# Pooled attention of four early head pairs with heads on halves of the partitions, and value blocks requested by ScalarE

## The chip, the cores and the metric

The kernel runs on one NeuronCore of one Trainium2 chip. The core has five engines with an instruction queue each, worked off in order: TensorE (PE, with its weight loads shown as PEld), VectorE (DVE), ScalarE (ACT), GpSimd (POOL) and SyncE (SP), which here only requests DMA transfers. The metric is the device time of one execution in microseconds, as the median of several runs.

## The reference

Inputs are q, k and v of shape 8 x 8 x 576 x 64 (batch, heads, positions, channels), a token mixing U (576 x 32) and V (32 x 576), and two feed-forward matrices (512 x 2048 and 2048 x 512), all float32.

```python
q_d = q.reshape(B, H, Sd, 4, D).mean(axis=3)      # k_d and v_d likewise, Sd = 144
out_d = sm_attn(q_d, k_d, v_d)                    # softmax attention of the pooled rows
out_up = np.repeat(out_d, 4, axis=2)
mask = np.abs(pos[:, None] - pos[None, :]) < 4
...                                               # softmax attention within the mask, with v
x = (out_up + out_local)                          # to B x S x 512
u = x + ((x.transpose(0, 2, 1) @ U) @ V).transpose(0, 2, 1)
return u + np.maximum(u @ w_ch1, 0.0) @ w_ch2
```

So each head has a pooled attention over 144 rows and a local one over a band of seven neighbours. Their sum is mixed over the tokens at rank 32, and a feed-forward network follows.

## The kernel before

Work is emitted as small operations to a planner (`Plan`, lines 55 to 200). Each operation has an engine, an estimated duration, what it reads and writes, and a priority. The planner simulates the five engines and one DMA stream, takes on each engine the ready operation of the lowest priority number, and emits all operations in the order of the simulated starts. On the chip each engine then follows that order, and waits where the data is not there yet. The estimates therefore set the order, and the chip sets the times.

Heads are handled in pairs, with the 64 channels of the first head on partitions 0 to 63 and those of the second on 64 to 127. Batch 0, the first four pairs, takes an "early" way that stays in on-chip memory (`early_global`, `local_blocks`, `early_mix`); the other 28 pairs take a "late" way through DRAM (`late_global`, `local_attn`, `mix_part`). The feed-forward (`ffn1`, line 941, and `ffn2`, line 966) runs over thirteen token tiles, four of 288 and nine of 384, in 16 slices of the hidden dimension each, and begins when batch 0 is mixed.

Pooled attention of an early pair (`early_global`, lines 442 to 514): GpSimd pools q, k and v (lines 437, 439, 454, 457). The 144 queries are cut in two groups of 72, which lie on 72 partitions. Line 468 makes the scores of both heads into two PSUM banks of the pool `ps_m`, which has two. Then for each head there are a maximum (475), a scaled copy of it (478) and two exponentials with sums (483); later, one head after the other, four transposes (497), a copy (501), the product with v (508) and a scaling (511) into `od`.

Local attention of an early pair (`local_blocks`) has band scores (line 609, on a mask laid by 621), a softmax (629 to 642), transposes (652, copied by 654), and the product with the value block `vw` (664), copied out by ACT as `ob` (668). There is one `vw` buffer for all four pairs, so that the request for a pair's block (`load_vw`, line 595) waits for line 664 of the pair before. All DMA requests stand in SP's queue.

`early_mix` brings `od` and `ob` under the channels (686, 687, 693), adds them (696), makes U's product (705 for the local part, 707 for the pooled part with a pooled U made once, lines 385 and 388), splits it (710, 711, 714) and applies V (723, 727). Lines 730 and 732 split the result into the two parts that the feed-forward reads.

Weights of the feed-forward come raw (line 414) and are converted by ACT (347), DVE (350, 352), ACT (358) and GpSimd (362), 32 of them, between all of this and the early part of the feed-forward. The first requests of batch 1 (gq, line 589) need the memory of the early buffers and wait until the last early operation has ended.

The late pooled attention (lines 537 to 577) puts the heads on halves of the partitions: three groups of 48 queries, head 0 on partitions 0 to 63 and head 1 on 64 to 127. Line 775 makes the scores in blocks of 32 queries, 541 takes the maximum of both heads, 543 and 545 follow, 556 transposes 128 x 128, and 559, 571 and 575 close it.

Of the kernel before, what the change touches and what calls it, by code (L numbers as in the profile page):

```python
# [203 lines left out]
def attn_mix_ffn_kernel(ctx: ExitStack, tc, q, kp, vp, qT, kT, v, U, Ub, V, w1, w2, band, eye, pool, vw, ident, outT):  # L204
# [30 lines left out]
    NOD = 3  # L235
# [7 lines left out]
    KV = vw.shape[2]  # L243

# [12 lines left out]
    def psum(pool, name, tag, bufs):  # L257
        return buf(pool, [128, 512], F32, name, tag, bufs)
# [48 lines left out]
    Upool = early_pool.tile([128, 2, 2 * R], F32, name="Upool")  # L307
# [65 lines left out]
    def load_ublk(prio):  # L373
        raw = raw_in(NFC - 1, "ubr")
        dma(lambda raw=raw: nc.sync.dma_start(
            out=raw().bitcast(U16)[:, :4 * NS * R - 1], in_=Ub.bitcast(U16)[:, 1:]), [], [raw], prio, 164)
        convert(raw, 128, NS * R, lambda: Ublk[:, :, 0:R], None, NS, "Ub", "cu", prio)
        pool_sb = buf(wts, [128, 144], F32, "pool", f"W2_{NFC - 5}:pool")
        dma(lambda: nc.sync.dma_start(out=pool_sb(), in_=pool), [], [pool_sb], prio, 74)
        pu = psum(ps_acc, "ps_p", "acc1:p", 1)  # L380
        u4 = lambda: pu()[:QH, :2 * R].rearrange("p (a r) -> p a r", a=2)

        def u_mm():
            for n, (r, a) in enumerate(CROSS):
                nc.tensor.matmul(u4()[:, a], pool_sb()[:, 64 - QL * r + QH * a:64 - QL * r + QH * a + QH], Ublk[:, r, 0:R],
                                 start=(n == 0), stop=(n == len(CROSS) - 1))
        op(PE, 0.7, u_mm, ["UbH", pool_sb], [pu], prio)
        act(2 * R, lambda: nc.scalar.activation(Upool[:QH, :, 0:R], u4(), AF.Copy), [pu], ["Up"], prio, 0.16)
# [43 lines left out]
    CROSS = ((0, 0), (1, 0), (2, 0), (2, 1), (3, 1), (4, 1))  # L432

# [8 lines left out]
    def early_global(b, hp, prio, qt, kt):  # L442
        sq = work(True, glo, [128, SD], F32, "smq")
# [3 lines left out]
        od = ring([2, 2, D], "od_e", NOD)  # L447
        vs = ring([4 * D], "vs_e")
# [12 lines left out]
        view = lambda t, n: t()[:QH, :2 * n].rearrange("p (a k) -> p a k", a=2)  # L461
        rs = work(True, glo, [QH, 2, 2], F32, "rs")
        ps = psum_pair(ps_m, "ps_s", "m:g", 2)

        def s_mm():
            for a in range(2):
                for hh, o in enumerate(heads):
                    nc.tensor.matmul(view(ps[hh], SD)[:, a], sq()[o, a * QH:(a + 1) * QH], sk()[o],
                                     start=True, stop=True)
        op(PE, pw(prio) * 1.4, s_mm, [sq, sk], ps, prio)  # L470
        Es = []
        for hh in range(2):
            p = ps[hh]
            mx = work(True, glo, [QH, 2], F32, "mx")
            dve(288, lambda p=p, mx=mx: nc.vector.tensor_reduce(
                out=mx(), in_=view(p, SD), axis=AX.X, op=ALU.max), [p], [mx], prio)
            nb = work(True, glo, [QH, 2], F32, "nb")
            act(2, lambda mx=mx, nb=nb: nc.scalar.activation(
                nb(), mx(), AF.Copy, scale=-1.0 / 128.0), [mx], [nb], prio, 0.16)
            E = ring([2, SD], "E_e")  # L480
            Es.append(E)
            for a in range(2):
                act(SD, lambda a=a, hh=hh, E=E, p=p, nb=nb: nc.scalar.activation(
                    E()[:QH, a, :], view(p, SD)[:, a, :], AF.Exp, bias=nb()[:, a:a + 1], scale=1.0 / 128.0,
                    accum_out=rs()[:, hh, a:a + 1]), [p, nb], [(E, a), (rs, a, hh)], prio, 0.237)
        rr = work(True, glo, [QH, 2, 2], F32, "rr")
        act(4, lambda: nc.scalar.activation(rr(), rs(), AF.Copy, bias=4e-9, scale=4.0),
            [(rs, a, hh) for a in range(2) for hh in range(2)], [rr], prio, 0.16)
        ri = work(True, glo, [QH, 2, 2], F32, "ri")
        dve(24, lambda: nc.vector.reciprocal(out=ri(), in_=rr()), [rr], [ri], prio)  # L490
        for hh in range(2):
            pt = psum(ps_m, "ps_t", "m:g", 2)

            def t_mm(hh=hh, pt=pt):
                for c in range(2):
                    for a in range(2):
                        nc.tensor.transpose(view(pt, SD)[:, c, a * QH:(a + 1) * QH],
                                            Es[hh]()[:QH, a, c * QH:(c + 1) * QH], ident_sb[:QH, :QH])
            op(PE, pw(prio) * 0.48, t_mm, [(Es[hh], 0), (Es[hh], 1), "ident"], [pt], prio)
            ET = Es[hh]  # L500
            act(288, lambda ET=ET, pt=pt: nc.scalar.activation(ET()[:QH], view(pt, SD), AF.Copy),
                [pt], [(ET, 0), (ET, 1)], prio, 0.05)
            pa = psum(ps_m, "ps_a", "m:g", 2)

            def a_mm(ET=ET, pa=pa, v=vsx[hh]):
                for a in range(2):
                    for c in range(2):
                        nc.tensor.matmul(view(pa, D)[:, a, :], ET()[:, c, a * QH:(a + 1) * QH],
                                         v()[:, c, :], start=(c == 0), stop=(c == 1))
            op(PE, pw(prio) * 0.95, a_mm, [(ET, 0), (ET, 1), vs], [pa], prio)  # L510
            dve(128, lambda pa=pa, hh=hh: nc.vector.tensor_tensor(
                out=od()[:QH, :, hh, :], in0=view(pa, D),
                in1=ri()[:, hh, :].unsqueeze(2).broadcast_to([QH, 2, D]), op=ALU.mult), [pa, ri], [(od, hh)], prio)
# [78 lines left out]
    def load_vw(b, h0, prio):  # L592
        vw_t = ring([NL + 2, D], "vw", 1)
        for hh in range(2):
            dma(lambda hh=hh: nc.sync.dma_start(
                out=vw_t()[hh * KW:hh * KW + KV, 0:NL], in_=vw[b * HP + h0 // 2, hh]), [], [(vw_t, hh)], prio, 221)
# [77 lines left out]
    def early_mix(b, hp, x, od, prio):  # L674
        rd = [(x, g) for g in range(2)] + [(od, g) for g in range(2)]
        up = lambda a: od()[:, a].rearrange("p h d -> p (h d)")
# [7 lines left out]
        def od_t():  # L684
            for a in range(2):
                nc.tensor.transpose(pc()[:, q4 - SD + a * QH:q4 - SD + (a + 1) * QH], up(a)[:QH], ident_sb[:QH, :QH])
            nc.tensor.transpose(pc()[:, :S - q4], flat(4)[:S - q4], ident_sb[:S - q4, :S - q4])
# [15 lines left out]
        def hu():  # L703
            for n in range(NS):
                nc.tensor.matmul(ph()[:2 * R, :2 * D], Ublk[:, n, :], flat(n), start=(n == 0), stop=False)
            for a in range(2):
                nc.tensor.matmul(ph()[:2 * R, :2 * D], Upool[:, a, :], up(a), start=False, stop=(a == 1))
        op(PE, 1.6, hu, rd + ["UbH", "Up"], [ph], prio)
# [34 lines left out]
    QC, NQ = 48, 3  # L743
# [345 lines left out]
```

## Time and profile before

| | us |
|---|---|
| median of three runs | 1007.88 |
| lowest and highest | 1006.73 and 1010.25 |
| profiled execution | 1009.96 |
| its span, first to last instruction | 1008.2 |
| busy in it: PE, DVE, ACT, POOL | 973.4, 440.4, 349.6, 572.3 |

The page gives busy time by engine, the chain of work that ended last (followed back from the end, each step to what released it), and groups of equal instructions with count, busy time, mean duration, idle time before them and what ended it. Views of the trace give stretches of time (windows), instructions in order of time, and waits by engine. `L664` is line 664 of the kernel. A matmul of float32 shows as two instructions, a transpose as one. A name ending in q, as SPq, is the queue of that engine, where DMA requests are issued.

The granted clock averages 0.99 over the span.

### The profile page before, as it was taken

How to read it: one execution, taken by the hardware profiler on the slowest of the kernel's cores; microseconds unless marked ns; L12 is line 12 of the kernel's file. 1: busy time of each engine (PE TensorE's matmuls, PEld its weight loads, DVE VectorE, ACT ScalarE, POOL GpSimd, SP SyncE). 2: the span in 40 equal slices, each digit the busy share in tenths (PEclk: the TensorE clock that was granted, in tenths of full speed). 3: DMA queues.
4: the chain of work that ended last, by engine and by line, in shares of the span. 5: the costliest groups of instructions: out<-in, count | busy, mean ns of one | idle time of the engine just before them, and what ended most of it. 6: DMA issues, size and time to landing. Idle time of an engine off the chain costs nothing.

```text
span 1008.2 us, 24256 instructions
## 1 busy us (share of the span) xinstructions
PE 973.4 (97%) x9724; PEld 944.7 (94%) x9724; DVE 440.4 (44%) x824; ACT 349.6 (35%) x1023; POOL 572.3 (57%) x641
## 2 busy tenths in 40 slices
PE   5979999799999999999999999999999999999998
PEld 4769899799899999999999999999999999999998
DVE  5666855535453543642635444454363222211211
ACT  5766644333343333432433333433331221111110
POOL 6677897867766764864867866766764111300100
PEclk9989999989999999999999999999999999999999
DMA  9678867656564645655554565465541021000000
GB/s 280 170 243 228 260 147 152 142 129 159 108 152 105 171 92 124 147 129 125 147 129 104 145 150 127 111 161 123 123 121 54 13 68 24 32 1 1 32 1 31
DMA packets 220648, 120.01 MB, mean 119 GB/s; under 512 B 173988, under 2 KB 196856, under 8 KB 220536
## 3 DMA queue, kind: packets, MB, share of 16 engines
q1 hardware_dynamic: 220536, 118.47, 47.2%
q8 instruction: 76, 1.25, 0.5%
q14 instruction: 36, 0.29, 0.1%
HBM read 87.57 MB, written 30.86 MB: 117 GB/s over the span
## 4 chain that ended last, share of the span: by engine, by line
PE 80%; DMA 4%; POOL 4%; DVE 2%; issue 1%; SPq 1%; ACT 1%; DVEq 0%; POOLq 0%
PE ps_h L941 36%; PE acc L966 35%; PE ps_a L571 2%; POOL Pt L837 2%; PE ps_b L775 2%; PE ps_hu L916 2%; DMA ul<-up_s 1%; PE ps_t L556 1%; PE ps_b L768 1%; DMA s_s<-se 1%; DVE acc L842 1%; PE ps_u L723 1%; POOL W L362 1%; DMA gT<-in_kT 1%; SPq L791 1%
## 5 line engine op out<-in xcount | busy, mean ns | idle before, releaser
L966 PE MATMUL acc<-hH,W 128*128 128x384 f32 (+1 forms) x1664 | 441.9, 327 | 0.0
L941 PE MATMUL ps_h<-uH,W 128*128 128x384 f32 (+1 forms) x1376 | 360.4, 324 | 5.3 <-DVE hL L950 5.3
L966 PEld LDWEIGHTS acc<-hH,W 128*128 128x128 f32 x1664 | 297.4, 188 | 2.2
L966 PE MATMUL acc<-hL,W 128*128 128x384 f32 (+1 forms) x832 | 268.2, 322 | 0.0
L837 POOL TENSOR_TENSOR Pt<-vl,ms 128x896 f32<-128x896 f32 (+1 forms) x140 | 239.4, 1789 | 43.9 <-DMA vl<-in_vp 23.9
L950 DVE SCALAR_TENSOR_TENSOR hL<-ps_h,hH 128x384 fp32r<-128x384 f32 (+1 forms) x208 | 109.1, 524 | 342.6 <-ACT hH L949 342.6
L941 PEld LDWEIGHTS ps_h<-uH,W 128*128 128x128 f32 x1376 | 246.4, 190 | 7.5 <-DVE hL L950 6.3
L949 ACT ACTIVATE hH<-ps_h 128x384 fp32r<-128x384 f32 (+1 forms) x208 | 97.2, 467 | 378.3 <-PE ps_h L941 370.3
L941 PE MATMUL ps_h<-uL,W 128*128 128x384 f32 (+1 forms) x688 | 221.6, 322 | 1.4 <-POOL uL L732 1.4
L842 DVE TENSOR_REDUCE acc<-Pt 128x128 f32<-128x1024 f32 (+1 forms) x140 | 152.8, 1107 | 55.0 <-POOL Pt L837 28.0
L966 PEld LDWEIGHTS acc<-hL,W 128*128 128x128 f32 x832 | 156.7, 188 | 0.0
L941 PEld LDWEIGHTS ps_h<-uL,W 128*128 128x128 f32 x688 | 130.8, 190 | 1.6 <-POOL uL L732 1.6
L941 PE MATMUL ps_h<-u,W 128*128 128x384 f32 x432 | 98.1, 334 | 0.0
L831 ACT ACTIVATE Pt<-ul 128x128 f32<-128x128 f32 (+1 forms) x140 | 55.6, 432 | 92.6 <-DVE acc L842 61.7
L908 POOL TENSOR_TENSOR xL<-xL,xH 116x640 fp32r<-116x640 f32 x28 | 44.0, 1570 | 67.1 <-ACT xH L907 55.5
L732 POOL TENSOR_TENSOR uL<-xT,uH 128x384 fp32r<-128x384 f32 (+2 forms) x52 | 40.9, 808 | 68.4 <-ACT uH L730 66.1
L976 POOL TENSOR_TENSOR o<-uH,uL 128x384 f32<-128x384 f32 (+1 forms) x43 | 38.9, 938 | 70.0 <-DMA out_t<-o 70.0
L941 PEld LDWEIGHTS ps_h<-u,W 128*128 128x128 f32 x432 | 76.9, 188 | 0.0
L531 POOL TENSOR_TENSOR vr<-vr 72x256 f32<-72x256 f32 x56 | 41.4, 740 | 31.2 <-DMA vr<-in_v 31.1
L362 POOL TENSOR_TENSOR W<-c,W 128x512 fp32r<-128x512 f32 x32 | 41.1, 1287 | 14.5 <-ACT W L358 14.5
L727 DVE TENSOR_TENSOR xT<-ps_u,xT 128x384 f32<-128x384 f32 (+2 forms) x64 | 27.3, 450 | 32.1 <-PE ps_u L723 31.9
L775 PE MATMUL ps_b<-smk,smq 64*32 64x144 f32 x672 | 38.6, 294 | 0.4 <-POOL smk L439 0.4
(131 smaller groups left out, 903.3 us busy)
## 6 DMA issues: line engine op xcount, KB each, us to landing
wr<-in_W SPq DMA_DIRECT2D x32, 511.8 KB
vl<-in_vp SPq DMA_DIRECT2D x56, 240.0 KB
vr<-in_v SPq DMA_DIRECT2D x64, 144.0 KB
gT<-in_kT SPq DMA_DIRECT2D x28, 291.0 KB
gq<-in_qT SPq DMA_DIRECT2D x28, 288.0 KB
up_s<-od SPq DMA_DIRECT2D x168, 48.0 KB
ul<-up_s SPq DMA_DIRECT2D x28, 288.0 KB
x_s<-acc SPq DMA_DIRECT2D x28, 288.0 KB
```

Source lines behind the costliest of these rows:

```text
L362: pool_tt(1.0 * n, lambda: nc.gpsimd.tensor_tensor(out=lo_out(), in0=ta()[l0:], in1=hi_out()[l0:].bitcast(F32), op=ALU.subtract), [t, *own ...
L531: pool_tt(256, lambda x=x: nc.gpsimd.tensor_tensor(out=x()[:, :, 0:2, :], in0=x()[:, :, 0:2, :], in1=x()[:, :, 2:4, :], op=ALU.add), [x], ...
L732: pool_tt(n, lambda uH=uH, uL=uL, uf=uf, us=us: nc.gpsimd.tensor_tensor(out=uL.ap(hp, us), in0=uf(), in1=uH.ap(hp, us).bitcast(F32), op=AL ...
L775: nc.tensor.matmul(pg()[m:m + QL, a * SD:(a + 1) * SD], sq()[o, n:n + QL], sk()[o], start=True, stop=True)
L831: act(n * D, lambda n=n, ps=ps, Pt=Pt: nc.scalar.activation(Pt()[:, :n, :, 7], ul()[:, ps, :], AF.Copy), [ul], [(Pt, 1)], prio, 0.16)
L837: nc.gpsimd.tensor_tensor(out=Pt()[:, :n, :, 0:7].rearrange("p s d o -> p o s d"), in0=win, in1=at()[:, ps, :].rearrange("p s o -> p o s") ...
L842: dve(8.5 * n * D, lambda n=n, ps=ps, Pt=Pt: nc.vector.tensor_reduce(out=acc()[:, ps, :], in_=Pt()[:, :n], axis=AX.X, op=ALU.add), [(Pt, 0 ...
L908: pool_tt(640, lambda: nc.gpsimd.tensor_tensor(out=xL(), in0=xL().bitcast(F32), in1=xH().bitcast(F32), op=ALU.subtract), [xL, xH], [xL], prio)
L941: nc.tensor.matmul(ps()[:, :tn], W1[fc]()[:, w, dc, :], u.ap(dc), start=(n == 0), stop=(n == 3 * NDC - 1))
L949: last_h[i] = act(tn, lambda: nc.scalar.activation(hH()[:, :tn], ps()[:, :tn], AF.Relu), [ps], [hH], FIRST, 0.05)
L950: dve(tn, lambda: nc.vector.scalar_tensor_tensor(hL()[:, :tn], ps()[:, :tn], 0.0, hH()[:, :tn].bitcast(F32), op0=ALU.max, op1=ALU.subtract ...
L966: nc.tensor.matmul(ac[e]()[:, :tn], W2[fc]()[:, w, es], hx()[:, :tn], start=(fc == 0 and n == 0), stop=(fc == NFC - 1 and n == 2))
```

## The change

The pooled attention of the four early pairs takes the form of the late one. Queries lie in three groups of 48, with the first head on partitions 0 to 47 and the second on 64 to 111; scores, maximum, exponentials, transposes, products and scaling are done for both heads at once. Scores need one PSUM bank, the transposes both, the product one. `smq` gets 16 zeroed columns, since blocks of 32 queries reach past the 48. `od` becomes two buffers of three groups (three of two groups before), and the products run over 72 rows, with no zeroed rest.

`early_mix` takes the pooled output from that form: six matmuls with the identity in place of two transposes, and six matmuls of 32 x 64 outputs in place of two of 64 x 128 for the pooled part of U's product, after the first local one. The pooled U has six blocks in two copies, one for each half of the partitions.

The value blocks of the second to the fourth pair are requested by ACT instead of SP.

```diff
-    NOD = 3
+    NOD = 2
...
+    QC, NQ = 48, 3
+    NP = 64 + QC
...
     for _ in range(2):
-        ring([2 * 2 * D], "vs_e")
-        ring([2, SD], "E_e")
+        ring([SD + 16], "smq_e")
         ring([NS, 2, KW], "ms_b", eng=nc.gpsimd)
...
-        op(PE, 0.7, u_mm, ["UbH", pool_sb], [pu], prio)
-        act(2 * R, lambda: nc.scalar.activation(Upool[:QH, :, 0:R], u4(), AF.Copy), [pu], ["Up"], prio, 0.16)
+        def l_mm():
+            for a in range(NQ):
+                for n, r in enumerate((3 * a // 2, 3 * a // 2 + 1)):
+                    for hh, m in enumerate((64, QC)):
+                        c = 64 - QL * r + QC * a
+                        nc.tensor.matmul(u3()[hh * 64:hh * 64 + m, a], pool_sb()[:, c:c + m], Ublk[:, r, 0:R],
+                                         start=(n == 0), stop=(n == 1))
+        op(PE, 0.7, l_mm, ["UbH", pool_sb], [pl], prio)
+        for hh in range(2):
+            act(NQ * R, lambda o=slice(hh * 64, hh * 64 + QC), hh=hh: nc.scalar.activation(
+                Upl[o, hh], u3()[o], AF.Copy), [pl], [f"Up{hh}"], prio, 0.16)
...
-        op(PE, pw(prio) * 1.4, s_mm, [sq, sk], ps, prio)
...
-            op(PE, pw(prio) * 0.48, t_mm, [(Es[hh], 0), (Es[hh], 1), "ident"], [pt], prio)
...
-            op(PE, pw(prio) * 0.95, a_mm, [(ET, 0), (ET, 1), vs], [pa], prio)
...
+            for a in range(NQ):
                 for c in range(2):
+                    for hh, o in enumerate(heads):
+                        m, n = hh * 64 + c * QL, a * QC + c * QL
+                        nc.tensor.matmul(ps()[m:m + QL, a * SD:(a + 1) * SD], sq()[o, n:n + QL], sk()[o],
+                                         start=True, stop=True)
+        op(PE, pw(prio) * 1.4, s_mm, [sq, sk], [ps], prio)
...
+        op(PE, pw(prio) * 1.1, t_mm, [(E, a) for a in range(NQ)] + ["ident"], pt, prio)
...
+        def a_mm():
+            for a in range(NQ):
+                for c in range(2):
+                    for hh in range(2):
+                        m, x = 64 - hh * (64 - QC), ((c * NQ + a) * 2 + hh) * QC
+                        nc.tensor.matmul(out()[hh * 64:hh * 64 + m, a, :], E()[:QH, x:x + m], vsx[hh]()[:, c, :],
+                                         start=(c == 0), stop=(c == 1))
+        op(PE, pw(prio) * 1.8, a_mm, [(E, "T", 0), (E, "T", 1), vs], [pa], prio)
...
-            dma(lambda hh=hh: nc.sync.dma_start(
-                out=vw_t()[hh * KW:hh * KW + KV, 0:NL], in_=vw[b * HP + h0 // 2, hh]), [], [(vw_t, hh)], prio, 221)
+            op(ACT if h0 else SP, 0.4, lambda hh=hh: (nc.scalar if h0 else nc.sync).dma_start(
+                out=vw_t()[hh * KW:hh * KW + KV, 0:NL], in_=vw[b * HP + h0 // 2, hh]), [], [(vw_t, hh)], prio,
+               move=0.01 + 221 / 290.0, lat=1.3)
...
-            for a in range(2):
-                nc.tensor.transpose(pc()[:, q4 - SD + a * QH:q4 - SD + (a + 1) * QH], up(a)[:QH], ident_sb[:QH, :QH])
-            nc.tensor.transpose(pc()[:, :S - q4], flat(4)[:S - q4], ident_sb[:S - q4, :S - q4])
+            nc.tensor.transpose(pc()[:, :128], flat(4), ident_sb)
+            for a in range(NQ):
+                for hh, o in enumerate(heads):
+                    r, c = slice(hh * 64, hh * 64 + QC), q4 - SD + a * QC
+                    nc.tensor.matmul(pc()[o, c:c + QC], od()[r, a], ident_sb[r, r], start=True, stop=True)
...
-                nc.tensor.matmul(ph()[:2 * R, :2 * D], Ublk[:, n, :], flat(n), start=(n == 0), stop=False)
-            for a in range(2):
-                nc.tensor.matmul(ph()[:2 * R, :2 * D], Upool[:, a, :], up(a), start=False, stop=(a == 1))
-        op(PE, 1.6, hu, rd + ["UbH", "Up"], [ph], prio)
+                nc.tensor.matmul(ph()[:2 * R, :2 * D], Ublk[:, n, :], flat(n), start=(n == 0), stop=(n == NS - 1))
+                for a in range(NQ if n == 0 else 0):
+                    for hh, o in enumerate(heads):
+                        nc.tensor.matmul(ph()[:R, o], Upl[:NP, hh, a], od()[:NP, a], start=False, stop=False)
+        op(PE, 1.6, hu, rd + ["UbH", "Up0", "Up1"], [ph], prio)
```

More of the change, by code (lines that the diff above doesn't have):

```diff
@@ L306, in attn_mix_ffn_kernel @@
     eye_sb = early_pool.tile([128, 128], BF16, name="eye_sb")
-    Upool = early_pool.tile([128, 2, 2 * R], F32, name="Upool")
+    Upl = early_pool.tile([128, 2, NQ, R], F32, name="Upl")
     Ublk = early_pool.tile([128, NS, 2 * R], F32, name="Ublk")
@@ L324, in attn_mix_ffn_kernel @@
     for _ in range(2):
-        ring([2 * 2 * D], "vs_e")
-        ring([2, SD], "E_e")
+        ring([SD + 16], "smq_e")
         ring([NS, 2, KW], "ms_b", eng=nc.gpsimd)
     ring([NL + 2, D], "vw", 1)
-    for _ in range(NOD):
-        ring([2, 2, D], "od_e", NOD, nc.gpsimd)
-    for k in ("vs_e", "E_e", "vw", "ms_b", "od_e"):
+    for k in ("smq_e", "vw", "ms_b"):
         kept[k][0] = 0
     nc.gpsimd.memset(Ublk[:, :, R:2 * R], 0.0)
-    nc.gpsimd.memset(Upool, 0.0)
+    nc.gpsimd.memset(Upl, 0.0)
     def convert(raw, pp, n, hi_out, lo_out, a, wkey, name, prio, own_bank=False, l0=0):
@@ L379, in load_ublk @@
         dma(lambda: nc.sync.dma_start(out=pool_sb(), in_=pool), [], [pool_sb], prio, 74)
[L380 to L386, printed above, removed]
-        op(PE, 0.7, u_mm, ["UbH", pool_sb], [pu], prio)
-        act(2 * R, lambda: nc.scalar.activation(Upool[:QH, :, 0:R], u4(), AF.Copy), [pu], ["Up"], prio, 0.16)
+        pl = psum(ps_acc, "ps_p", "acc1:p", 1)
+        u3 = lambda: pl()[:, :NQ * R].rearrange("p (a r) -> p a r", a=NQ)
+        def l_mm():
[9 more added lines that the diff above has]
+                Upl[o, hh], u3()[o], AF.Copy), [pl], [f"Up{hh}"], prio, 0.16)
     def load_u(prio):
@@ L442, in early_global @@
     def early_global(b, hp, prio, qt, kt):
-        sq = work(True, glo, [128, SD], F32, "smq")
+        sq = ring([SD + 16], "smq_e")
         sk = work(True, glo, [128, SD], F32, "smk")
@@ L446, in early_global @@
         pool_halves(kt, (SPAD - S) // 2, sk, True, prio)
-        od = ring([2, 2, D], "od_e", NOD)
-        vs = ring([4 * D], "vs_e")
+        od = buf(early_pool, [128, NQ, D], F32, "od_e", None, NOD)
+        vs = buf(early_pool, [QH, 4 * D], F32, "vs_e", None, 2)
         x = (buf(early_pool, [QH, 2, 2, 4, D], F32, "vr") if b else
@@ new lines, in early_global @@
+        rs, rr, ri, mx, nb = (buf(early_pool, [128, NQ], F32, n + "_e", None, 2) for n in ("rs", "rr", "ri", "mx", "nb"))
+        E = buf(early_pool, [128, 2 * NQ * 2 * QC], F32, "E_e", None, 2)
+        Ea = lambda: E()[:, 0:NQ * SD].rearrange("p (a k) -> p a k", a=NQ)
+        ET = lambda: E()[:QH].rearrange("p (c a h q) -> p c a h q", c=2, a=NQ, h=2)
+        ps = psum(ps_m, "ps_s", "m:g", 2)
+        def s_mm():
+            for a in range(NQ):
+                for c in range(2):
+                    for hh, o in enumerate(heads):
+                        m, n = hh * 64 + c * QL, a * QC + c * QL
+                        nc.tensor.matmul(ps()[m:m + QL, a * SD:(a + 1) * SD], sq()[o, n:n + QL], sk()[o],
+                                         start=True, stop=True)
@@ new lines, in early_global, with t_mm @@
+        act(NQ, lambda: nc.scalar.activation(rr(), rs(), AF.Copy, bias=4e-9, scale=4.0),
+            [(rs, a) for a in range(NQ)], [rr], prio, 0.16)
+        dve(8 * NQ, lambda: nc.vector.reciprocal(out=ri(), in_=rr()), [rr], [ri], prio)
+        pt = psum_pair(ps_m, "ps_t", "m:g", 2)
+        def t_mm():
+            for c in range(2):
+                for a in range(NQ):
+                    nc.tensor.transpose(pt[c]()[:QH, a * 128:(a + 1) * 128], Ea()[:, a, c * QH:(c + 1) * QH], ident_sb)
+        op(PE, pw(prio) * 1.1, t_mm, [(E, a) for a in range(NQ)] + ["ident"], pt, prio)
@@ new lines, in early_global @@
+        for c in range(2):
+            act(2 * NQ * QC, lambda c=c: nc.scalar.activation(
+                ET()[:, c], pt[c]()[:QH, 0:128 * NQ].rearrange("p (a h q) -> p a h q", a=NQ, h=2)[..., 0:QC], AF.Copy),
+                [pt[c]], [(E, "T", c)], prio, 0.05)
+        pa = psum(ps_m, "ps_a", "m:g", 2)
+        out = lambda: pa()[:, :NQ * D].rearrange("p (a d) -> p a d", a=NQ)
+        def a_mm():
+            for a in range(NQ):
+                for c in range(2):
+                    for hh in range(2):
+                        m, x = 64 - hh * (64 - QC), ((c * NQ + a) * 2 + hh) * QC
+                        nc.tensor.matmul(out()[hh * 64:hh * 64 + m, a, :], E()[:QH, x:x + m], vsx[hh]()[:, c, :],
+                                         start=(c == 0), stop=(c == 1))
@@ L674, in early_mix @@
     def early_mix(b, hp, x, od, prio):
-        rd = [(x, g) for g in range(2)] + [(od, g) for g in range(2)]
-        up = lambda a: od()[:, a].rearrange("p h d -> p (h d)")
+        rd = [(x, g) for g in range(2)] + [od]
         flat = lambda n: x()[:, n].rearrange("p h d -> p (h d)")
@@ L741, in load_padded @@
             nc.sync.dma_start(out=t[hh * 64:(hh + 1) * 64].rearrange("p s d -> p (s d)"), in_=w)
-    QC, NQ = 48, 3
     NH = NL // 2
```

57 lines of the change are left out of this document (10 added, 47 removed).

## The prediction

> **What bounds the kernel now.** I read the page's first and fourth parts, then windows of four microseconds over the start, then the timeline of TensorE and the waits of each engine there.
>
> ```profile
> PE 973.4 (97%) x9724; PEld 944.7 (94%) x9724; DVE 440.4 (44%) x824; ACT 349.6 (35%) x1023; POOL 572.3 (57%) x641
> ...
> PE 80%; DMA 4%; POOL 4%; DVE 2%; issue 1%; SPq 1%; ACT 1%; DVEq 0%; POOLq 0%
> ```
>
> TensorE (PE) is busy 97% of the span and holds 80% of the chain that ended last. So the total is PE's feed-forward work plus what PE loses, and the losses that this change can touch lie in the first 62 us, when batch 0 is prepared and the feed-forward has not begun.
>
> ```profile
> 24.00:28.00 4.00, 2.64 (x19) 2.56 (x19) 2.79 (x7) 2.17 (x7) 4.00 (x5) 1.00 1.02 278
> ...
> 40.00:44.00 4.00, 3.90 (x45) 3.36 (x36) 3.12 (x7) 3.71 (x11) 1.60 (x3) 1.00 0.74 164
> 44.00:48.00 4.00, 3.20 (x100) 2.27 (x98) 3.42 (x10) 3.67 (x14) 1.94 (x2) 1.00 0.24 88
> 48.00:52.00 4.00, 3.69 (x19) 3.24 (x20) 2.23 (x5) 3.59 (x14) 1.97 (x4) 0.64 0.98 269
> ...
> 64.00:68.00 4.00, 0.82 (x3) 0.59 (x4) 3.37 (x6) 3.05 (x6) 4.00 (x7) 0.77 1.00 311
> ```
>
> The columns are the stretch, its length, then busy time of PE, its weight loads, DVE, ACT and POOL, the granted clock, the DMA share and GB/s. From 40 to 52 PE and ACT are both nearly full (10.8 and 11.0 of 12 us). At 64 to 68 PE stands almost still. The early stage is thus a mixed pipeline: no single engine is full all the time, and the order of five in-order queues sets the pace.
>
> ```profile
> 32.03 1.24 PE L468 MATMUL ps_s<-smk,smq 64*72 64x144 f32 x8
> 39.08 1.04 PE L664 MATMUL ps_ba<-vw,et 38*32 38x64 f32 x80
> 40.04 0.44 PE L497 MATMUL ps_t<-ident_sb,E_e 72*72 72x72 f32 x4
> 42.04 0.67 PE L508 MATMUL ps_a<-vs_e,E_e 128*72 128x64 f32 x8
> 42.75 0.29 DVE L511 TENSOR_TENSOR od_e<-ps_a,ri 72x128 f32<-72x128 f32 x1 [0.41 <-PE ps_a L508]
> 44.54 0.71 PE L468 MATMUL ps_s<-smk,smq 64*72 64x144 f32 x8
> 53.73 0.42 PE L497 MATMUL ps_t<-ident_sb,E_e 72*72 72x72 f32 x4
> 55.81 0.28 DVE L511 TENSOR_TENSOR od_e<-ps_a,ri 72x128 f32<-72x128 f32 x1
> ```
>
> Pooled scores (L468) of the third and the fourth pair are 12.5 us apart. The fourth pair's start at 44.54 comes 1.5 us after the third pair's second head is scaled (42.75 to 43.04), because two heads hold both general PSUM banks. Also the same eight score matmuls take 1.24 us at 32 and 0.71 at 44: PE runs at half pace in the first 36 us, though the granted clock says 1.00 there. A matmul added early costs double.
>
> **The change part by part.** The span is 1008.2 us and the profiled execution 1009.96, 1.8 us of it around the span; the median of the three runs is 1007.88, 2.1 us below the profiled one. The sum below is a difference and is put on the median.
>
> The new form is the one that the later pairs use already, so their groups price it (the first seven rows); the other rows are the old form.
>
> ```profile
> L775 PE MATMUL ps_b<-smk,smq 64*32 64x144 f32 x672 | 38.6, 294 | 0.4 <-POOL smk L439 0.4
> L545 ACT ACTIVATE E<-ps_b,nb 128x144 f32<-128x144 f32 x84 | 31.1, 377 | 0.8
> L571 PE MATMUL ps_a<-vs,E 72*64 72x64 f32 (+1 forms) x672 | 26.5, 228 | 0.5 <-DVE xT L727 0.5
> L556 PE MATMUL ps_t<-ident_sb,E 128*72 128x128 f32 x168 | 22.9, 273 | 2.3 <-DVE xT L727 2.3
> L559 ACT ACTIVATE E<-ps_t 72x288 f32<-72x288 f32 x56 | 19.9, 406 | 5.2 <-PE ps_t L556 4.5
> L541 DVE TENSOR_REDUCE mx<-ps_b 128x3 f32<-128x432 f32 x28 | 17.0, 607 | 16.6 <-PE ps_b L768 16.2 <-PE ps_b L775 0.4
> L575 DVE TENSOR_TENSOR od<-ps_a,ri 112x192 f32<-112x192 f32 x28 | 9.9, 352 | 8.6 <-PE ps_a L571 8.4
> L483 ACT ACTIVATE E_e<-ps_s,nb 72x144 f32<-72x144 f32 x16 | 5.8, 369 | 0.1
> L475 DVE TENSOR_REDUCE mx<-ps_s 72x2 f32<-72x288 f32 x8 | 3.3, 448 | 2.0 <-PE ps_s L468 2.0
> L501 ACT ACTIVATE E_e<-ps_t 72x288 f32<-72x288 f32 x8 | 3.2, 404 | 4.1 <-PE ps_t L497 4.0
> L707 PE MATMUL ps_hu<-od_e,Upool 128*64 128x128 f32 x16 | 2.4, 274 | 0.0
> L385 PE MATMUL ps_p<-Ublk,pool 128*72 128x32 f32 x12 | 1.7, 309 | 0.0
> L478 ACT ACTIVATE nb<-mx 72x2 f32<-72x2 f32 x8 | 1.6, 201 | 2.1 <-DVE mx L475 2.0
> L686 PE MATMUL ps_c<-ident_sb,od_e 72*128 72x72 f32 x8 | 1.4, 258 | 0.0
> ```
>
> VectorE: two maxima and two scalings a pair, 2 x 0.448 + 2 x 0.286 = 1.47 us, become one of each, 0.607 + 0.352 = 0.96. That is 0.51 less a pair, 2.0 in all.
>
> ScalarE: four exponentials, two nb and two ET copies, 4 x 0.369 + 2 x 0.201 + 2 x 0.404 = 2.69, become 3 x 0.377 + one 0.201 + 2 x 0.406 = 2.14. That is 0.55 less a pair, 2.2 in all. Against it stand a second copy of the pooled U (0.22, the old one's time) and six DMA requests. No trace shows a request on ACT; the same pair of requests on SP takes 0.80 us (first row of the next fence), so 0.4 each, 2.4 in all, between 0 and twice that. ACT's work is thus about the same, +0.4, but the third and the fourth pair's requests fall behind L664 at 40 and 47, where ACT is full: 2 x 0.8 less 2 x 0.55 = **+0.5** on the path.
>
> TensorE: old scores, transposes and products of a warm pair take 0.71 + 2 x 0.43 + 2 x 0.67 = 2.91. New: transposes 22.9 / 28 = 0.82, products 26.5 / 28 = 0.95, scores between 0.71 and 38.6 / 28 = 1.38 (that group runs among 72 dense matmuls); I take 1.0, together 2.77. Moving the pooled output under the channels takes 12 short matmuls in place of two transposes: 12 x 0.95 / 24 = 0.48 against 1.4 / 4 = 0.35. Its part in hu takes 12 of 64 columns in place of 4 of 128: 0.48 to 12 x 0.67 / 8 = 1.0 against 0.60; I take 0.6, nearer L571, whose matmuls are as short. Net per pair 0.0, ends -0.4 and +0.8. The pooled U (L385) goes from 12 instructions to 24 on two halves of the columns: its 1.7 us stays or doubles, I take +0.4, nearer the low end because L571's 0.04 us an instruction against L508's 0.08 shows halves overlapping. Two cold pairs count double, so the ends are six times the pair's, and with the pooled U: PE **+0.4**, ends -2.4 and +6.5.
>
> Chain: the second head's transposes, copy, products and scaling go (28.12 to 30.94 of the second pair, then 40.04 to 43.04 and 53.73 to 56.09: 2.8, 3.0 and 2.4 us, 8.2 together), and the next pair's scores need one free bank instead of two.
>
> ```profile
> 40.06 0.80 SPq L595 DMA_DIRECT2D vw<-in_vw  x2
> ...
> 28.12 0.69 PE L497 MATMUL ps_t<-ident_sb,E_e 72*72 72x72 f32 x4
> ...
> 30.65 0.29 DVE L511 TENSOR_TENSOR od_e<-ps_a,ri 72x128 f32<-72x128 f32 x1 [0.26 <-PE ps_a L508]
> ...
> 25.36 0.34 PE L609 MATMUL ps_b<-kd,qt 64*32 64x38 f32 x3 [2.72 <-issue]
> ...
> 35.38 0.63 PE L707 MATMUL ps_hu<-od_e,Upool 128*64 128x128 f32 x4
> ...
> 61.15 0.28 DVE L711 TENSOR_TENSOR stk<-ps_hu,stk 32x128 fp32r<-32x128 f32 x1
> ...
> 62.09 0.33 SPq L589 DMA_DIRECT2D gq<-in_qT  x1
> ...
> PE ps_u L723 <- DVE stk L711: 2.2, 3, 1.4
> PE ps_hu L705 <- DVE xT L696: 0.8, 1, 0.8
> ...
> SPq L595 <- PE ps_ba L664: 12.0, 2, 8.0
> ...
> ACT half L347 <- DMA wr<-in_W: 2.5, 1, 2.5
> ```
>
> PE fills these stretches with other work; from 20 to 62 it lost only 2.7 us without a named releaser (L609) and 3.0 us to VectorE (L723, L705). Of the 8.2 I count the share of the 42 us in which PE stands by these waits, 5.7 / 42 = 14%, **-1.2**, between 0 and all; next late is ob, the local output of the same pair, which L664 must give first. Of VectorE's 3 us I count half, **-1.5**, as 0.51 us a pair leaves its queue ahead of stk and xT.
>
> SP's queue: requests of v blocks waited 12.0 us for L664 with the weight requests behind them. Moved to ACT, SP goes on. I cost that at **0**: up to 62 no conversion waited for its weights (ACT's waits from 20 to 62 name only PE and DVE), and the requests behind gq wait for the early buffers until 62.09 anyway. If weights come sooner after that too, the most to win is L347's 2.5 us, its wait for weights in 62 to 72. The wait itself now stands on ACT: behind it are uH, the ET copies and et. But the two ob copies ahead of it on ACT wait for the same L664, so it adds nothing as long as the planner keeps that order.
>
> In the Trainium skill, DMA: Bandwidth & Descriptors, section "Issuing engines are not separate DMA queues", requests of all engines run on the same 16 DMA engines and interleave, so another issuing engine saves only issue time. By that rule the block itself comes no sooner and the 0 stands; no trace here has two issuers.
>
> The memsets of vs_e, E_e and od_e go and smaller ones come, all while the first loads are under way: 0. Two od buffers for three: the third pair's last products stand at 42.04 (L508), the first pair's hu has ended at 36.0 (L707): 0.
>
> Sum: 0.5 + 0.4 - 1.2 - 1.5 = -1.8. Feed-forward and batch 1 start that much earlier; 1007.9 - 1.8 gives **1006.1 us**.
>
> **The rivals.**
>
> *The banks pace the stage.* If the 12.5 us between pooled scores is what holds the pairs apart, the 8.2 us come off in full: -8.2 + 0.5 + 0.4 = -7.3, 1000.6 us. For it: L468 starts right behind the last od. Against: PE is busy 3.9 of 4 us there, and local blocks (L664) must follow too.
>
> *TensorE gets too many small matmuls (slower).* Instructions per pair go from 49 to 89 matmuls, each with a weight load. PE stood 2.7 us amid 72 equal matmuls (L609, until 25.36), with DMA engines full (1.02) and no releaser; I read that as instructions arriving late. One more such stop, with half of PE's upper end, is 2.7 + 3.2 = +5.9, 1012.0 us. It decides as soon as the stop falls in 25 to 56, where PE is packed. Switching the array's tile shape adds four switches a pair; at most the time of one matmul (0.27, L556) each, 16 x 0.27 = 4.3, it gives 1006.1 + 4.3 = 1010.4 by itself, inside this rival. The Trainium skill, TensorEngine Tiling, section "Key Properties", says that changing the tiling mode drains TensorE, which speaks for this; the later pairs' rows, which already have such switches inside, show no idle before them except the named waits.
>
> *ScalarE stalls on the request.* If the plan puts a request ahead of ob, or the block's earlier transfer is late, ACT inherits a part of SP's wait; the second one was 12.0 - 8.0 = 4.0 us: 1006.1 + 4.0 = 1010.1 us.
>
> *Nothing comes through*, since a gain in the start is eaten at 64 to 68 behind weight conversions: 1007.9, inside the forecast's own range.
>
> **How the numbers follow.** Forecast 0.44 (1006.1, own range 1003 to 1009), banks 0.24, small matmuls 0.23, request 0.09. What a measurement tells from no change is about 0.3%, 3.0 us: faster means below 1004.9, slower above 1010.9. Faster: 0.24 and three tenths of the forecast, 0.37. Slower: most of 0.23 and a third of 0.09, 0.22. Same: 0.41. The range takes in the banks' and the small matmuls' times with about one us beyond each: 999.5 to 1013.
>
> **What would show it.** Right: pooled scores closer than 12.5 us; L711's last before 61.15 us; SP's wait for L664 gone; no ACT wait at its requests. Wrong: a PE wait without releaser in 25 to 56, an ACT wait for L664 ahead of ob. A different order of the plan after 62 can move the losses at 64 to 72 either way, which I cannot see from here.

## The result, and the profile after

| | before | changed |
|---|---|---|
| median of six runs | 1009.44 us | 1015.47 us |
| lowest and highest | 1006.73 and 1013.02 | 1012.47 and 1017.60 |
| ratio, 95% interval | | 1.0062, 1.0032 to 1.0091 |
| profiled execution, its span | 1009.96, 1008.2 | 1016.62, 1014.8 |

The changed kernel is about 6 us slower. Measured once more it came to 1.0050 (1.0023 to 1.0077). The forecast was 1006.1 us in a range of 999.5 to 1013: the time moved the other way and lies outside.

The first and the fourth part of the page after, busy time by engine and the chain that ended last:

```profile
PE 980.2 (97%) x9896; PEld 946.8 (93%) x9896; DVE 437.8 (43%) x814; ACT 347.4 (34%) x1012; POOL 569.9 (56%) x638
...
PE 83%; POOL 6%; DMA 4%; SPq 2%; DVE 2%; issue 2%; ACT 1%; ACTq 0%; POOLq 0%; DVEq 0%
```

The first number points to TensorE. PE was busy 973.4 of 1008.2 us before and 980.2 of 1014.8 after. Its idle time is 34.8 us before and 34.6 after. So the 6.6 us of span are no more waiting in sum: PE is busy 6.8 us longer. Of these, 4.3 us are more work and 2.5 us more time at half clock (the work column below, 957.8 against 953.5). VectorE and ScalarE did become shorter, by 2.6 and 2.2 us, and nothing of it reached the end.

Where the idle time lies has changed. Windows over two stretches of the trace before (stretch, length, then busy time of PE, weight loads, DVE, ACT, POOL, granted clock, DMA share, GB/s):

```profile
0.00:85.00 85.00, 65.48 (x1095) 56.30 (x1096) 55.27 (x126) 54.68 (x160) 54.97 (x80) 0.94 0.77 228
85.00:300.00 215.00, 203.38 (x2445) 197.70 (x2444) 118.32 (x220) 92.51 (x276) 168.44 (x182) 0.98 0.67 161
```

The same of the trace after:

```profile
0.00:85.00 85.00, 60.72 (x1185) 48.04 (x1185) 48.56 (x107) 47.64 (x132) 50.79 (x72) 0.88 0.71 217
85.00:300.00 215.00, 210.45 (x2506) 204.79 (x2507) 118.94 (x223) 95.47 (x287) 164.73 (x179) 0.98 0.66 162
```

PE stands still for 24.3 us of the first 85 (19.5 before), but only for 4.6 us from 85 to 300 (11.6 before). The early stage ends far later, and PE then idles less. The tile `stk`, whose writing ends each early pair, has this row in the view by tile after (the times are starts; the last one was at 61.2 before):

```profile
L711 DVE TENSOR_TENSOR stk<-ps_hu,stk x4: 282/282/282, 28.3 to 70.8; 32x128 fp32r<-32x128 f32 x4
```

The first pair came 8.3 us earlier than before (36.6), the last 9.6 us later. Between the two stands a conspicuous hole. Windows of four microseconds after:

```profile
36.00:40.00 4.00, 0.00 (x0) 0.00 (x0) 0.57 (x1) 0.23 (x2) 1.13 (x2) 0.93 1.03 404
40.00:44.00 4.00, 3.35 (x109) 2.74 (x108) 1.94 (x6) 1.25 (x3) 2.96 (x4) 0.50 1.04 411
44.00:48.00 4.00, 4.00 (x24) 3.15 (x23) 2.06 (x4) 2.25 (x6) 1.36 (x2) 0.50 0.98 263
```

And the timeline of SP and of PE there (start, duration, instruction, idle time before it):

```profile
29.11 12.52 SPq L418 DMA_DIRECT2D wr<-in_W  x10
...
40.05 0.34 PE L607 MATMUL ps_b<-kd,qt 64*32 64x38 f32 x8 [4.24 <-issue]
```

From 36 to 40 us PE does nothing and the other engines little, the DMA engines are full, PE has no releaser, and then the clock is granted at a half. SP, which before waited for the product with the v block, now sends ten weight requests in a row. This suggested the first theory; the second was PE's work.

### The profile page after: what moved, and what is told of

Read it like the earlier page. It is cut to its first block, busy times and chain, and to the rows that moved or that the text cites. A ratio compares the mean times of both kernels' runs of the same rounds, so it can differ in the third digit from the quotient of the medians.

```text
span 1014.8 us, 24556 instructions
## 1 busy us (share of the span) xinstructions
PE 980.2 (97%) x9896; PEld 946.8 (93%) x9896; DVE 437.8 (43%) x814; ACT 347.4 (34%) x1012; POOL 569.9 (56%) x638
## 4 chain that ended last, share of the span: by engine, by line
PE 83%; POOL 6%; DMA 4%; SPq 2%; DVE 2%; issue 2%; ACT 1%; ACTq 0%; POOLq 0%; DVEq 0%
PE ps_h L940 36%; PE acc L965 35%; POOL Pt L836 3%; PE ps_a L568 2%; DMA vr<-in_v 2%; PE ps_b L774 2%; PE ps_t L554 1%; PE ps_b L767 1%; PE ps_hu L915 1%; SPq L578 1%; PE ps_u L723 1%; PE ps_hu L704 1%; SPq L790 1%; DVE acc L841 1%; DVE o L978 1%
## 5 line engine op out<-in xcount | busy, mean ns | idle before, releaser
L732 POOL TENSOR_TENSOR uL<-xT,uH 128x384 fp32r<-128x384 f32 (+2 forms) x52 | 40.9, 808 | 63.6 <-ACT uH L730 61.0
```

The lines of the kernel that those rows point to most:

```text
L732: pool_tt(n, lambda uH=uH, uL=uL, uf=uf, us=us: nc.gpsimd.tensor_tensor(out=uL.ap(hp, us), in0=uf(), in1=uH.ap(hp, us).bitcast(F32), op=AL ...
```

## Experiments

Each kernel is compared with the kernel before on the same chip, with 7 to 12 executions of its own; three chips were used. Theory 1: the weight requests that run ahead cost the time. Theory 2: the pooled form costs it, by TensorE's work. Theory 3: the planner's new order costs it. Four kernels came first.

```diff
  first: the changed kernel, order as planned
-            op(ACT if h0 else SP, 0.4, lambda hh=hh: (nc.scalar if h0 else nc.sync).dma_start(
+            op(ACT if h0 else SP, 0.4, lambda hh=hh: nc.sync.dma_start(
  second: the kernel before, order as planned
-            dma(lambda hh=hh: nc.sync.dma_start(
+            dma(lambda hh=hh: (nc.scalar if h0 else nc.sync).dma_start(
  third: the changed kernel with load_vw of the kernel before, planned anew
  fourth: the kernel before with load_vw of the changed kernel, planned anew
```

> The changed kernel, every engine's order as it is, only the six requests of the v blocks of the second to fourth pair stand on SP again, at their place in the plan. TensorE, VectorE and GpSimd run the same instructions in the same order as after; ScalarE has six requests (2.2 us) less. Theory 1 (requests run ahead: with the v blocks on ACT nothing holds SP, ten weight requests fill the DMA engines from 29 to 48 us, and TensorE's instruction packets, the v blocks and the q and k loads come late): SP waits for the product with the v block again, the ten requests in a row break up, the stop of TensorE at 36 to 40 us goes or falls below 1.5 us, the last stk is written at 64 us or earlier instead of 70.8, and the time falls by 5 us or more from the changed kernel's 1015.5, to 1004 to 1010. Theory 2 (the pooled form itself costs the time: more and smaller matmuls on a TensorE at half pace): within 2 us of 1015.5, stk at 69 to 71. Theory 3 (the planner's new order costs it): within 2 us of 1015.5 too, but with the stop at 36 to 40 gone and DMA no longer full.

> The kernel before, every engine's order as it was, old pooled form; only the six requests of the v blocks of the second to fourth pair stand on ACT. Theory 1: eight weight requests run in a row on SP, DMA is full from about 30 to 45 us, TensorE gets a stop with no releaser and restarts after an instruction packet, stk's last comes at 64 to 70 us (before 61.2), and the time rises by 3 to 7 us to 1012 to 1016. Theory 2 and theory 3: as before, 1007 to 1011, stk at 60 to 62.

> The pooled form with heads on halves alone: the changed kernel with the loader of the v blocks as before (planned and issued on SP), so the planner makes an order of its own. Theory 1: 1003 to 1009, stk's last at 55 to 62 us, since the first pair is 8 us earlier and nothing takes it back. Theory 2: 1013 to 1017 with stk at 68 to 71. Theory 3: anywhere, apart from the first experiment by more than 3 us although both have their requests on SP.

> The requests alone: the kernel before with the changed loader (planned and issued on ACT), old pooled form, an order of the planner's own with eleven weight requests in a row on SP. Theory 1: slower than before by 3 to 8 us, 1012 to 1017, with DMA full from 29 to 50 us and a stop of TensorE of 3 us or more without a releaser in it. Theory 2: 1007 to 1011. Theory 3: apart from the second experiment by more than 3 us.

Measured: first 1.0042 (1.0022 to 1.0063), second 1.0054 (1.0031 to 1.0078), third 1.0031 (1.0006 to 1.0057), fourth 1.0013 (0.9989 to 1.0037). No theory came through alone. In the order of before the requests' place costs 5.4 us, as theory 1 wanted. But with the requests back on SP the changed kernel stays slow, as theories 2 and 3 wanted, although the long stop is gone (PE is busy 3.55 of the 4 us from 36 to 40); its last stk still ends at 69.6. The pooled form alone is slower than before, against theory 1's gain, and the requests alone (fourth), where theory 1 wanted 3 to 8 us, cannot be told from no change.

The next four complete the table of form, planning and engine, repeat the changed kernel, and take work away from PE.

```diff
  fifth: the fourth kernel, order as planned
-            op(ACT if h0 else SP, 0.4, lambda hh=hh: (nc.scalar if h0 else nc.sync).dma_start(
+            op(ACT if h0 else SP, 0.4, lambda hh=hh: nc.sync.dma_start(
  sixth: the third kernel, order as planned
-            dma(lambda hh=hh: nc.sync.dma_start(
+            dma(lambda hh=hh: (nc.scalar if h0 else nc.sync).dma_start(
  seventh: the third kernel
-                for a in range(NQ if n == 0 else 0):
+                for a in range(0):
```

> The changed kernel again, unaltered, beside the next three on one chip. If its first measurement holds: 1.003 to 1.009 of before, a stop of TensorE of 2 us or more between 34 and 42 us behind an instruction packet, stk's last at 69 to 72 us.

> The kernel of the fourth experiment (old pooled form, planned with the requests on ScalarE), every engine's order as it is, but the six requests are emitted on SP. Against before it has only another order; against the fourth experiment only another place of the requests. Theory 1 (place of the requests costs 2 to 6 us in either order): 2 to 5 us below the fourth experiment, 0.996 to 1.000 of before. Theory 2 (what costs is TensorE's added work, 3.9 us at full clock, and here is none of it): 0.998 to 1.002 of before. Theory 3 (the order): 1.003 or more of before.

> The kernel of the third experiment (new pooled form, planned with the requests on SP), every engine's order as it is, but the six requests are emitted on ScalarE. Theory 1: 2 to 6 us above the third experiment, 1.005 to 1.009 of before, ten weight requests in a row on SP. Theory 2: as the third, 1.002 to 1.005. Theory 3: as the third.

> The kernel of the third experiment without the pooled output's part of the hidden products (the matmuls of Upl and od_e, 12 records a pair, 48 in all, 4.4 us of busy time there); that part of the result is left out. Theory 2 (work of TensorE in the early stage counts in full): 3 to 5 us below the third experiment, 0.998 to 1.001 of before. If that work lies in time that TensorE loses anyway, by waits or at half clock: within 1.5 us of the third experiment.

Measured: changed kernel again 1.0050 (1.0023 to 1.0077), with the hole again, at 34.2 to 38.6 us; fifth 1.0011 (0.9987 to 1.0034); sixth 1.0037 (1.0014 to 1.0059); seventh 0.9999 (0.9979 to 1.0019). Without the pooled part of the hidden products the new form is level with before. Its 4.7 us of busy time in the third kernel (row of L706 there; L707 after), 2.3 us of work at full clock by the table below, brought 0.0032, about 3.2 us. The interval of that difference is some 0.003 to either side, so it excludes little more than zero by itself.

The last four test both remaining claims by dose: requests on ScalarE with SP still held by a small piece, and more TensorE work in the kernel before.

```diff
  eighth (kernel before) and ninth (changed kernel), in load_vw
+            def request(hh=hh):
+                o, w = vw_t()[hh * KW:hh * KW + KV], vw[b * HP + h0 // 2, hh]
+                k = NL - 1 if h0 else NL
+                if h0:
+                    nc.sync.dma_start(out=o[:, k:NL], in_=w[:, k:NL])
+                (nc.scalar if h0 else nc.sync).dma_start(out=o[:, 0:k], in_=w[:, 0:k])
  tenth and eleventh, in od_t of the kernel before (15 in the eleventh)
-            for a in range(2):
+            for a in (0, 1) * 7:
                 nc.tensor.transpose(pc()[:, q4 - SD + a * QH:q4 - SD + (a + 1) * QH], up(a)[:QH], ident_sb[:QH, :QH])
```

> The second experiment (kernel before, six requests of the v blocks on ScalarE, 1.0054 of before) with one addition: SP requests the last of each block's 18 positions itself, so it waits for the product with the block before as it did, and holds its weight requests behind that wait; ScalarE requests the other 17. Theory 1 (the weight requests that run ahead cost the time): back to 0.998 to 1.002 of before, weight requests at 40 us and later again behind the third pair's block. If ScalarE's own six requests cost it (2.2 us of its time, ahead of ob copies): stays at 1.004 to 1.007.

> The changed kernel with the same addition: SP requests the last position of each block and so waits, ScalarE requests the rest. Theory 1: as the first experiment, 1.002 to 1.006 of before, no stop of TensorE of 4 us between 34 and 42 us. If the requests' cost in the changed kernel is ScalarE's own time: as the changed kernel, 1.005 or more.

> The kernel before, every engine's order as it is, with the two small transposes of the pooled output done seven times in each pair of batch 0: 48 more TensorE records in the early stage, about 4 us more of busy time at the 0.1 us each that the group of 8 takes; the result is the same. Theory 2 (work of TensorE in the early stage is paid in full): 3 to 5 us slower, 1.003 to 1.005 of before. If such work is hidden by waits: 0.999 to 1.002.

> The same with the two transposes done fifteen times: 112 more records, about 9 us more of busy time. Theory 2: 6 to 10 us slower, 1.006 to 1.010 of before, and more than the run before it. If hidden: 0.999 to 1.003.

Measured: eighth 1.0019 (0.9999 to 1.0039), ninth 1.0058 (1.0036 to 1.0081), tenth 1.0044 (1.0021 to 1.0067), eleventh 1.0074 (1.0045 to 1.0104).

The tenth and the eleventh give the price of TensorE's work. Their row of the transposes in the groups of instructions (1.4 us for 8 in the kernel before); the tenth:

```profile
L686 PE MATMUL ps_c<-ident_sb,od_e 72*128 72x72 f32 x56 | 5.1, 253 | 0.0
```

and the eleventh:

```profile
L686 PE MATMUL ps_c<-ident_sb,od_e 72*128 72x72 f32 x120 | 9.8, 249 | 0.0
```

3.7 us more busy time cost 0.44%, 4.4 us (2.1 to 6.8 by its interval); 8.4 us more cost 0.74%, about 7.4 us (4.5 to 10.5). Nothing else was changed, and no engine's order. TensorE's work in the early stage is paid about in full, though PE stands idle for nearly 20 of the first 85 us in all three kernels (19.5 before, 20.4 and 19.8).

All kernels together. "Work" is PE's busy time with each moment counted by the clock granted in it, and by a half before the first clock record of the trace (35.4 us in the kernel before, 22.4 after), so it estimates busy time at full clock. The half before that record is read from equal matmuls: the scores of a pair after (L474) take 1.66 us at 7.7 and 18.5 us, and 0.94 at 28.3. The weight is a little too low for small matmuls, whose time does not quite double.

| kernel | form | planned for | requests by | ratio | work, us | last stk ends, us |
|---|---|---|---|---|---|---|
| before | old | SP | SP | 1 | 953.5 | 61.4 |
| second | old | SP | ACT | 1.0054 | 952.8 | 64.3 |
| eighth | old | SP | ACT, piece by SP | 1.0019 | 955.0 | 59.0 |
| fourth | old | ACT | ACT | 1.0013 | 953.5 | 68.5 |
| fifth | old | ACT | SP | 1.0011 | 954.6 | 66.4 |
| third | new | SP | SP | 1.0031 | 956.7 | 68.2 |
| sixth | new | SP | ACT | 1.0037 | 959.8 | 69.7 |
| changed, twice | new | ACT | ACT | 1.0062, 1.0050 | 957.8, 957.7 | 71.1, 71.1 |
| ninth | new | ACT | ACT, piece by SP | 1.0058 | 959.6 | 70.4 |
| first | new | ACT | SP | 1.0042 | 957.0 | 69.6 |
| seventh | new, part left out | SP | SP | 0.9999 | 954.4 | 63.4 |
| tenth | old, 48 records more | SP | SP | 1.0044 | 957.6 | 63.6 |
| eleventh | old, 112 records more | SP | SP | 1.0074 | 963.0 | 65.5 |

Work separates the forms without overlap: 952.8 to 955.0 old, 956.7 to 959.8 new, means 953.9 and 958.1, so the form adds 4.2 us. That hangs on the half before the first record: counted in full there, the forms overlap and the means are 1.9 us apart. Times follow: kernels that differ in the form alone, or in it and the order that it leads to, stand 0.31% (third less before), -0.17 (sixth less second), 0.43 (changed, mean of two, less fourth), 0.31 (first less fifth) and 0.39 (ninth less eighth) apart. The mean is 0.25%, 2.5 us, each of the five uncertain by about 0.3 and the mean by some 0.1, as they scatter. The tenth, with work as in the new form and none of its other parts, has the time of the new form.

The end of the early stage is no measure of the time. The fourth ends it 7 us later than before and costs 0.13%; the second ends it 3 us later and costs 0.54%.

**The requests.** Only in the order of before does their place show. The timeline of SP in the second kernel, where eight weight requests are sent in a row:

```profile
30.11 9.74 SPq L414 DMA_DIRECT2D wr<-in_W  x8
```

and in the eighth, where SP waits for the product again and the requests stand apart:

```profile
37.67 0.80 SPq L599 DMA_DIRECT2D vw<-in_vw  x2
38.51 0.42 SPq L414 DMA_DIRECT2D wr<-in_W  x1
44.62 0.78 SPq L599 DMA_DIRECT2D vw<-in_vw  x2
45.44 3.59 SPq L414 DMA_DIRECT2D wr<-in_W  x5
```

ScalarE makes all six requests in both, so its own time is no cause of the difference: 0.35% (0.0054 less 0.0019, uncertain by 0.3) goes with SP's wait, and so most likely with the weights that run ahead. How they cost it is not shown. In the one profile of the second kernel work is 952.8, no more than before, and PE's idle time 36.2 us, 1.4 more, while PE is busy 978.0 us, 4.6 more: most of the loss there is time at half clock. In the changed kernel the same repair does nothing. Windows of the ninth kernel:

```profile
36.00:40.00 4.00, 2.92 (x164) 2.48 (x166) 3.35 (x9) 2.67 (x8) 3.71 (x6) 0.94 0.29 110
40.00:44.00 4.00, 3.35 (x57) 2.71 (x40) 1.63 (x5) 1.96 (x5) 3.06 (x4) 0.50 0.48 109
```

The hole at 36 to 40 is gone, DMA has room, and the last stk still ends at 70.4 and the time is 1.0058. The most conspicuous hole of the trace was not the price, within the 0.3% that these runs can tell.

**What stays open.** The form explains 2.5 to 4.2 us of the 5 to 6. For the rest, the four old-form kernels with another order or another place of the requests average 0.24% above before. That fits a loss by disturbing the order of before, but apart from the second none of them is separated from no change, and in the changed kernel the share of the requests (first and ninth against it, 0.14% less and nothing) is below what these runs can tell. No kernel that computes everything was faster than before.

A rival for the rest is the clock, and no run changes it alone. Over all executions the mean granted clock of the changed kernel is 0.981 against 0.986 of before on the same chip; the first and the ninth, which share its order, lie 0.4 and 0.6% below before too, and the seventh, which is level with before in time, does not. The fifth, 0.35% below at a time of 1.0011, fits less well. Half a percent of the clock is 5 us where PE is busy throughout. The mean takes the time before the first clock record as full, so it is rough.

## Why the prediction failed, point by point

**TensorE at +0.4.** This is the step that failed. The prediction put the net change of a pair at 0.0 (ends -0.4 and +0.8); the work column, of whole kernels, gives 4.2 us for the four pairs and the pooled U together, about +1 a pair. It took the new hidden products (L707) at 0.6 a pair as before, and the moving of the output at 0.48. Groups of instructions after (busy time, mean ns of one, idle time before them):

```profile
L707 PE MATMUL ps_hu<-od_e,Upl 112*32 112x64 f32 x48 | 5.3, 291 | 0.0
L474 PE MATMUL ps_s<-smk,smq_e 64*32 64x144 f32 x96 | 5.3, 369 | 0.3 <-POOL smk L441 0.2
L492 PE MATMUL ps_t<-ident_sb,E_e 128*72 128x128 f32 x24 | 4.7, 317 | 2.2 <-ACT E_e L481 2.2
L506 PE MATMUL ps_a<-vs_e,E_e 72*64 72x64 f32 (+1 forms) x96 | 4.6, 248 | 0.4 <-ACT E_e L495 0.4
L686 PE MATMUL ps_c<-ident_sb,od_e 48*64 48x48 f32 x48 | 2.9, 267 | 0.0
L387 PE MATMUL ps_p<-Ublk,pool 128*64 128x32 f32 (+1 forms) x24 | 1.1, 220 | 1.2 <-DVE xT L695 0.8 <-issue 0.4
```

The three groups before that the prediction did not show:

```profile
L468 PE MATMUL ps_s<-smk,smq 64*72 64x144 f32 x32 | 4.4, 420 | 0.5 <-POOL smk L439 0.5
L497 PE MATMUL ps_t<-ident_sb,E_e 72*72 72x72 f32 x32 | 4.5, 280 | 1.9 <-ACT E_e L483 1.9
L508 PE MATMUL ps_a<-vs_e,E_e 128*72 128x64 f32 x64 | 7.6, 281 | 1.1 <-POOL vs_e L457 1.1
```

The hidden products went from 2.4 to 5.3 us, and the moving from 1.4 to 2.9. Scores and transposes added 1.1, the products with v gave 3.0 back and the pooled U 0.6, so the six rows go from 22.0 to 23.9 us. In the third kernel the six rows sum to 24.7. But a row mixes clocks and counts what its group overlaps with others. The hidden products alone, in windows around one pair each (stretch, length, busy time of PE and of weight loads, granted clock, DMA share, GB/s), after:

```profile
25.00:28.00 3.00, 0.86 (x12) 0.70 (x12) 1.00 0.90 210
45.00:48.00 3.00, 1.49 (x12) 1.25 (x12) 0.50 0.96 216
```

and before:

```profile
43.00:46.00 3.00, 0.60 (x4) 0.46 (x4) 1.00 0.55 157
```

Three of the four pairs after take 1.49 us, all or nearly all at half clock; before, all four take 0.60 to 0.63. So at full clock a pair's hidden products cost 0.86 us, 0.26 more, and most of the row's growth is where half-clock time fell. The moving takes 0.55 us at full clock against 0.29, 0.26 more where the prediction put 0.13. The two are 2.1 us over four pairs, half of the 4.2. Scores, transposes and products, taken at 2.77 a pair, came to 2.7 in the third pair after and 3.3 in the fourth. How the rest splits is not shown, as the groups overlap.

The prediction judged the hidden products by L571, "whose matmuls are as short". Those are two heads on separate halves of the array and overlap: 0.91 us for 24 in the third pair after, 0.04 each. L707 spans 112 rows and both heads, one after the other: 0.86 for 12, 0.07 each. The upper end, 0.67 / 8 a matmul, was nearer. With 4.2 in place of 0.4 and nothing for the two savings below, the prediction's sum would be 0.5 + 4.2 = +4.7 us, against 6.2 and 5.0 measured.

**The second head's round at -1.2 and VectorE's queue at -1.5.** Neither reached the time. Waits of PE from 12 to 72 us after (total, times, longest):

```profile
PE ps_b L607 <- issue: 5.3, 2, 4.2
PE ps_bt L650 <- ACT ob L666: 2.1, 2, 1.5
PE ps_c L682 <- ACT uH L730: 1.4, 1, 1.4
PE ps_u L723 <- DVE stk L711: 1.0, 1, 1.0
PE ps_hu L704 <- DVE xT L695: 0.4, 1, 0.4
```

The two waits on VectorE that the prediction named did fall, from 3.0 to 1.4 us, about as forecast. But waits for ScalarE's ob and uH rose from 0.7 to 3.5, and the stops without a releaser from 2.7 to 5.3. PE's idle time in the first 85 us rose from 19.5 to 24.3 us, and in no kernel with the whole new form is it below before's (third 20.8, ninth 19.8). Work that left ACT and DVE saved nothing here: another wait took the place of the one that shrank.

**ScalarE's requests at +0.5.** Not seen, and not excluded: the trace has no wait of ACT at its requests, and the eighth kernel, with all six on ACT, is 1.0019 (0.9999 to 1.0039).

**SP's queue at 0.** Wrong in the order of before, where moving the requests costs 0.54%. The prediction asked only whether a conversion would get its weights sooner, not what the wait of SP had held back. In the changed kernel the step cannot be told from 0. The block itself came no sooner, as the prediction held: the third pair's was requested at 41.7 us after and at 40.1 before. No run here tests the rule that the prediction cited for it, by which another issuing engine saves only issue time (the Trainium skill, DMA: Bandwidth & Descriptors, section "Issuing engines are not separate DMA queues").

**The rivals.** The slower one, small matmuls, named both the mechanism and the stop: it took half of TensorE's upper end and one more stop, 1012.0. On before's three runs, 1.0062 is 1014.1. It had the right direction and mechanism and a chance of only 0.23, since the working put the likeliest cost of TensorE at its low side. The stop that it counted at 2.7 us came, with 4.2, and did not decide. What switches of the array's shape cost was not measured apart. *The banks* did not pace the stage: scores now need one bank, the third pair's came 9.8 us after the second's, the fourth's 21.1 us after the third's, and the time rose. *ScalarE stalls on the request* did not happen: the third pair's request (41.72 us) stood behind its first ob copy (41.62), which had waited 5.4 us for the product. *Nothing comes through* also holds in part: the 8.3 us that the first pair gained were lost by the second, and PE idled 7.0 us less from 85 to 300.

**The signs.** Stk's last came at 70.8 instead of before 61.15, and PE had two stops without a releaser, 5.3 us: both pointed to wrong. Pooled scores (L474) came closer in two of three steps (10.8 and 9.8 us) and 21.1 us apart in the last. SP's wait for the product was gone and ACT had none at its requests, the signs of right, and they said nothing of the time.

## What to carry to other kernels

Where one engine is busy 97% of the span, price a change first by what it adds to that engine, instruction group by instruction group, even where the engine idles around it; savings on the others count for nothing until a run shows them. Price new small matmuls by a row with the same number of array rows and the same overlap, not by one of the same length, and compare rows at the same clock. A request that waits in a queue also holds back what stands behind it: before it is moved, list what it lets loose. And a large hole in the trace, or a stage that ends late, is a suspect and no price: repair it alone and time it.

## What the runs showed of the hardware

**TensorE's stops without a releaser end behind an instruction packet, and the longest come while DMA is full.** The DMA view from 37 to 38 us after, packets by queue with their share of the 16 engines:

```profile
q1 hardware_dynamic: 112, 0.41, 101.5%
q8 instruction: 1, 0.02, 6.8%
```

In this stop PE restarted 1.5 us after its instruction packet of 16 KB had ended (37.5 + 1.1, restart at 40.05). The fourteen traces have eighteen stops of PE of 1 us or more without a releaser, the 2.7 us at L609 that the prediction quotes among them, and each ends 1.3 to 1.7 us after such a packet. In fifteen the DMA share is 0.97 or more, and the longest lasts 4.4 us; the three with 0.05 to 0.55 last 1.8 us at most. That PE waits for the instructions in the packet is read from this distance; the profile does not name it. In the second kernel the profile puts such a stop down to a ScalarE exponential (L636) of the local attention, which had ended 0.8 us before the restart and whose tile the product does not read:

```profile
40.01 0.66 PE L693 MATMUL ps_x<-ident_sb,ob 128*128 128x128 f32 x4
42.40 1.22 PE L508 MATMUL ps_a<-vs_e,E_e 128*72 128x64 f32 x8 [1.73 <-ACT ms_b L636]
```

There the packet ran from 39.9 to 41.0. The Trainium skill, Runtime: NRT & Kernel Launch, section "Instruction fetch mechanics", has the cost of refilling instructions "mostly hidden". These traces differ: it was not hidden in these stops, though the ninth kernel, which lacks the one at 36 to 40 us and is no faster, shows that a stop need not decide the time.

**Half-clock time follows the long stop, and comes without one.** After the 4.2 us without a matmul the granted clock was 0.50 for 10.2 us (39.4 to 49.6), with PE busy 4.00 of 4.00 from 44 to 48. The ninth kernel, without that stop, has 0.50 from 40 to 44 too. Falls in all traces last 3.4 us or a multiple, but for the last of each, which the end of the trace cuts. The Trainium skill, TensorE: Matmul & The Clock Gate, section "What's actually happening", has the gate decide by free-running windows of 3413 ns; the lengths of the falls agree with it. Where such a fall lands differs from trace to trace of nearly equal kernels, so one profile's busy time compares only after weighting by the clock, as in the work column.
